# Second half of q copied by ScalarE alone, and one of two barriers at the program's end left out

## Chip, cores, metric

One core of one Trainium2 chip. The metric is the device time of one execution in microseconds, as the median of several runs; the profile's span runs from the first to the last instruction of the program and is some 1.8 us shorter.

## The reference

A decode step: one token for each of four sequences. Layer norm, then attention with 32 heads over the last 2048 rows of a cache, and a gated feed-forward block beside it. Cut to what matters:

```python
x = A_x                                   # (4, 1, 640)
xn = _layernorm(x, axis=-1)
# _A_ref: q = xn @ wq; W = 2048, Dh = 192, 32 heads
k = k_cache[:, :, Sk - W:, :]; v = v_cache[:, :, Sk - W:, :]
scores = jnp.einsum("bhqd,bhkd->bhqk", q, k) * (Dh ** -0.5)
o = jnp.einsum("bhqk,bhkd->bhqd", softmax(scores), v)
# ... o @ wo
# _B_ref: silu(xn @ w1) * (xn @ w3) @ w2
return x + _A_ref(xn, ...) + _B_ref(xn, ...)
```

K, V and the weights are 223 MB in bf16, each byte used once.

## The kernel before

All large loads go out from one sequencer (SP) in a fixed order. K has two buffers, so the load for head h+2 waits until VectorE has multiplied all of head h:

```python
def load_k(h):
    kt = kpool.tile([P, NJ, Dh], BF16, tag="kt")          # KBUFS = 2
    nc.sync.dma_start(out=..., in_=k_win[:, h]...)
```

q is projected in two halves of six 512-column blocks, in six PSUM banks; each half is copied to SBUF by ScalarE and VectorE in turn:

```python
for c0 in range(0, NQ, 6):                                # NQ = 12
    qps = [...six PSUM tiles...]
    ...                                                   # PE: 5 x 6 matmuls
    for i, qp in enumerate(qps):
        dst = qbc[:, (c0 + i) * QC:(c0 + i + 1) * QC]
        if i % 2:
            nc.vector.tensor_copy(out=dst, in_=qp[:])
        else:
            nc.scalar.copy(out=dst, in_=qp[:])
for i in range(2):                                        # banks of blocks 2 and 3
    o_ps = ps_o.tile([P, 2 * Dh], FP32, tag="o_ps", name="o_ps")
    nc.vector.memset(o_ps[:], 0.0)
...
def mult(u):                                              # VectorE, 128 times
    nc.vector.tensor_tensor(out=pr[:], in0=kts[h][:, ...], in1=qbc[:, h * Dh:(h + 1) * Dh]..., op=ALU.mult)
```

Behind the kernel's last instruction the framework puts an end block. From the program's listing, shortened (four engines signal POOL, which releases them; each barrier is eleven instructions):

```text
SP    drain, waits for all engines and all DMA queues
ACT/PE/DVE/SP  drain, gather+1 ; wait release      first barrier
POOL  drain ; wait gather>=4 ; release+4
POOL  drain ; EVENT_SEMAPHORE_RANGE_CLEAR
ACT/PE/DVE/SP  drain, gather+1 ; wait release      second barrier
POOL  drain ; wait gather>=4 ; release+4
```

Of the kernel before, what the change touches and what calls it, by code (L numbers as in the profile page):

```python
# [34 lines left out]
def first_load_first(nc):  # L35


    for f in nc.python_module().functions:
        head, body = f.blocks[0], f.blocks[1]
        sp = mybir.EngineType.SP  # L40
        i, ins = next((i, ins) for i, ins in enumerate(body.instructions)
                      if ins.engine == sp and not isinstance(ins, mybir.InstNoOp))
        assert isinstance(ins, mybir.InstDMACopy) and not ins.has_wait()
        j = next(j for j, other in enumerate(head.instructions)
                 if other.engine == sp and isinstance(other, mybir.InstDrain))
        del body.instructions[i]
        head.instructions.insert(j, ins)


@with_exitstack  # L50
def kernel(
# [19 lines left out]
    nc = tc.nc  # L71
# [26 lines left out]

    nc.at_finalize(keep_loaded_weights)
    nc.at_finalize(first_load_first)  # L100
    ctx.enter_context(tc.manual_schedule())
    head = ctx.enter_context(tc.tile_pool(name="head", bufs=1))
    fpool = ctx.enter_context(tc.tile_pool(name="ffn", bufs=1))
# [134 lines left out]
    for c0 in range(0, NQ, 6):  # L238
        qps = [pool.tile([P, QC], FP32, tag=tag, name="qps")
               for pool, tag in ((ps_add, "ps"), (ps_add, "ps"), (ps_o, "o_ps"), (ps_o, "o_ps"), (ps_m, "mt"), (ps_t, "t"))]  # L240
        for kc in range(KC):
            for i, qp in enumerate(qps):
                nc.tensor.matmul(qp[:], lhsT=xnT[:, kc].rearrange("p a b -> p (a b)"),  # L243
                                 rhs=wq_rows[kc][:, (c0 + i) * QC:(c0 + i + 1) * QC],
                                 start=(kc == 0), stop=(kc == KC - 1))
        for i, qp in enumerate(qps):
            dst = qbc[:, (c0 + i) * QC:(c0 + i + 1) * QC]
            if i % 2:
                nc.vector.tensor_copy(out=dst, in_=qp[:])  # L249
            else:  # L250
                nc.scalar.copy(out=dst, in_=qp[:])
# [322 lines left out]
```

## Time and profile before

| | before |
|---|---|
| time, median of 3 runs | 525.95 us (525.63 to 526.19) |
| span of the profiled run | 523.8 us |
| busy share PE / VectorE / ScalarE | 69% / 65% / 11% |
| DMA load queue busy | 99.2% |

The last pieces of the chain of waits (start, length, what):

```profile
489.68 30.66 DMA w<-in_B_w_dram
...
520.38 0.76 PE acc L264 x8
521.13 0.47 DVE res L542
```

The large last part of w2 (480 KB), issued at 489.68, lands at 520.34. Behind the loads come only the last sums, the result's copy, its store and the end block. The timeline's row of SP issuing the first K load that has to wait for a buffer:

```profile
41.62 0.54 SPq L125 DMA_DIRECT2D kt<-in_A_k_cache_dram  x1
```

### The profile page before, as it was taken

What the parts mean: (1) busy time and instruction counts of PE and PEld (TensorE: products, weight loads), DVE (VectorE), ACT (ScalarE), POOL (GpSimd) and SP (SyncE); (2) the same over time, 40 slices, a digit from 0 to 9 for tenths busy, and PEclk for the clock granted to TensorE, in tenths of its full rate; (3) what the DMA queues carried; (4) which work ended last, traced back from release to release, by engine and by line L of the source; (5) the groups of instructions that cost most, each with busy time, mean ns of one, the idle gap of its engine ahead of it and who ended that gap; (6) DMA issues with size and microseconds to landing.
All of it is one profiled execution on the core that took longest, in us unless ns stands there. A gap on an engine that the chain in (4) does not pass through costs nothing.

```text
span 523.8 us, 4820 instructions
## 1 busy us (share of the span) xinstructions
PE 361.8 (69%) x2336; PEld 75.9 (14%) x1643; DVE 340.9 (65%) x413; ACT 55.8 (11%) x176; POOL 5.6 (1%) x12
## 2 busy tenths in 40 slices
PE   0965866887668776667547768586686876675685
PEld 0100111121111111111111111111111111111122
DVE  3268853687656767577646877466667766667671
ACT  2111111111001110101100111001101110011111
POOL 4000000000000000000000000000000000000000
PEclk9979886898878998789997988889878898889988
DMA  9999999999999999999999999999999999999996
GB/s 389 422 443 425 433 431 432 428 433 432 430 435 428 437 418 446 424 437 426 434 434 429 432 434 429 435 427 435 425 437 434 427 437 431 430 434 425 441 418 275
DMA packets 11904, 223.26 MB, mean 426 GB/s; under 512 B 1332, under 2 KB 1608, under 8 KB 3052
## 3 DMA queue, kind: packets, MB, share of 16 engines
q1 hardware_dynamic: 11868, 222.96, 99.2%
q8 instruction: 15, 0.25, 0.2%
q14 instruction: 5, 0.04, 0.0%
q10 hardware_dynamic: 16, 0.01, 0.0%
HBM read 222.96 MB, written 0.01 MB: 426 GB/s over the span
## 4 chain that ended last, share of the span: by engine, by line
DMA 60%; PE 20%; DVE 15%; ACT 3%; issue 1%; SPq 1%
DMA kt<-in_A_k_cache_dram 44%; PE ps L288 11%; DMA w<-in_B_w_dram 11%; DVE pr L277 10%; DMA vt<-in_A_v_cache_dram 5%; PE po L361 4%; PE qps L243 3%; DVE sc L296 2%; ACT ex L324 1%; DVE z L332 1%; DMA x_sb<-in_A_x_dram 1%; PE mt L318 1%; ACT L324 0%; ACT negm L321 0%; PE mt L305 0%
## 5 line engine op out<-in xcount | busy, mean ns | idle before, releaser
L288 PE MATMUL ps<-pr,idb 128*128 128x512 bf16 x768 | 214.7, 422 | 137.6 <-DVE pr L277 137.5
L277 DVE TENSOR_TENSOR pr<-kt,qbc 128x3072 bf16<-128x3072 bf16 x128 | 223.5, 1746 | 104.0 <-DMA kt<-in_A_k_cache_dram 104.0
L296 DVE TENSOR_REDUCE sc<-ps 128x16 f32<-128x512 f32 x128 | 87.1, 681 | 2.7 <-PE ps L288 2.6
L340 PE MATMUL o_ps<-vt,z 128*8 128x384 bf16 x1024 | 60.5, 380 | 0.2 <-DVE z L332 0.2
L361 PE MATMUL po<-o_sb,sel_w 128*32 128x192 f32 x128 | 49.2, 518 | 0.6 <-ACT o_sb L343 0.6
L340 PEld LDWEIGHTS <-z 128*8 128x8 bf16 x1024 | 26.2, 95 | 98.8 <-issue 89.2
L332 DVE TENSOR_TENSOR z<-ex,mask_b 128x256 bf16<-128x256 bf16 x32 | 13.5, 423 | 38.6 <-ACT ex L324 38.6
L343 ACT COPY o_sb<-o_ps 128x384 f32<-128x384 f32 x32 | 15.3, 478 | 196.9 <-PE o_ps L340 196.9
L313 ACT ACTIVATE gneg<-gmax 1x128 f32<-1x128 f32 x32 | 9.8, 308 | 162.8 <-DVE gmax L310 162.8
L305 PEld LDWEIGHTS mt<-idf,lmax 128*1 128x1 f32 x32 | 3.2, 101 | 127.5 <-issue 125.5
L361 PEld LDWEIGHTS po<-o_sb,sel_w 128*32 128x32 f32 x128 | 13.8, 130 | 29.4 <-issue 27.9
L288 PEld LDWEIGHTS <-idb 128*128 128x128 bf16 x124 | 12.0, 97 | 39.3 <-issue 32.8
L318 PEld LDWEIGHTS mt<-ones_ff,gneg 1*128 1x128 f32 x64 | 9.6, 186 | 47.1 <-issue 43.7
L243 PE MATMUL qps<-wt,xnT 128*128 128x512 bf16 x59 | 14.9, 412 | 0.1
L318 PE MATMUL mt<-ones_ff,gneg 1*128 1x1 f32 x64 | 12.3, 259 | 0.7 <-ACT gneg L313 0.7
L321 ACT COPY negm<-mt 128x1 f32<-128x1 f32 x32 | 5.1, 159 | 70.4 <-PE mt L318 70.4
L310 DVE TENSOR_REDUCE gmax<-mt 1x4 f32<-1x128 f32 x32 | 8.8, 274 | 5.8 <-PE mt L305 5.8
L348 PEld LDWEIGHTS po<-rsum,tot_w 128*32 128x32 f32 x64 | 4.4, 108 | 51.5 <-ACT ex L324 35.4
L249 DVE CAST qbc<-qps 128x512 bf16<-128x512 f32 x6 | 3.8, 684 | 11.7 <-PE qps L243 11.7
L324 ACT ACTIVATE ex<-sc,negm 128x64 bf16<-128x64 f32 x32 | 11.1, 348 | 1.0
L305 PE MATMUL mt<-idf,lmax 128*1 128x128 f32 x32 | 10.9, 340 | 0.0
L199 PE MATMUL xnT_ps<-idb,xn 4*128 4x4 bf16 x5 | 0.4, 178 | 13.4 <-DVE xn L194 13.4
(74 smaller groups left out, 84.4 us busy)
## 6 DMA issues: line engine op xcount, KB each, us to landing
kt<-in_A_k_cache_dram SPq DMA_DIRECT2D x32, 3072.0 KB, 19.1
vt<-in_A_v_cache_dram SPq DMA_DIRECT2D x32, 3072.0 KB, 25.5
wo_t<-in_A_wo_dram SPq DMA_DIRECT2D x8, 960.0 KB, 20.7
wt<-in_A_wq_dram SPq DMA_DIRECT2D x2, 3072.0 KB
w<-in_B_w_dram SPq DMA_DIRECT2D x1, 1920.0 KB
wt<-in_A_wq_dram SPq DMA_DIRECT2D x1, 1536.0 KB, 19.5
w<-in_B_w_dram SPq DMA_DIRECT2D x1, 1536.0 KB
w<-in_B_w_dram SPq DMA_DIRECT2D x2, 640.0 KB
```

What stands on the lines that cost most here:

```text
L243: nc.tensor.matmul(qp[:], lhsT=xnT[:, kc].rearrange("p a b -> p (a b)"), rhs=wq_rows[kc][:, (c0 + i) * QC:(c0 + i + 1) * QC], start=(kc == ...
L277: nc.vector.tensor_tensor(out=pr[:], in0=kts[h][:, g * JQ:(g + 1) * JQ, :], in1=qbc[:, h * Dh:(h + 1) * Dh].unsqueeze(1).to_broadcast([P, ...
L288: nc.tensor.matmul(ps[:], lhsT=idb[:], rhs=pr[:, :, kk * DD:(kk + 1) * DD], start=(kk == 0), stop=(kk == NK - 1))
L296: nc.vector.tensor_reduce(out=scs[h][:, g * JQ:(g + 1) * JQ], in_=pss.pop(u)[:], axis=AX.X, op=ALU.add)
L305: nc.tensor.transpose(out=mt[0:1, 0:P], in_=chs[h][0][:], identity=idf[:])
L313: nc.scalar.activation(out=gneg[:], in_=gmax[:].unsqueeze(1).to_broadcast([1, PB, B]), func=ACTF.Copy, scale=-SCALE)
L318: nc.tensor.matmul(mt[:, P:P + 1], lhsT=gneg[:].rearrange("o p b -> o (p b)"), rhs=ones_ff[:], start=True, stop=True)
L324: nc.scalar.activation(out=ex[:], in_=scs.pop(h)[:], func=ACTF.Exp, bias=negm[:, 0:1], scale=SCALE, accum_out=rsum[:])
L332: nc.vector.tensor_tensor(out=z[:], in0=ex[:].unsqueeze(2).to_broadcast([P, NJ, B]), in1=mask_b[:].unsqueeze(1).to_broadcast([P, NJ, B]), ...
L340: nc.tensor.matmul(o_ps[c * CT:c * CT + 2 * B, :], lhsT=z[:, 2 * jj:2 * jj + 2, :], rhs=vt[:, 2 * jj:2 * jj + 2, :], start=(jj < 4), stop= ...
L343: nc.scalar.copy(out=o_sb[:], in_=o_ps[:])
L361: nc.tensor.matmul(po[sl, 0:Dh], lhsT=sel_w[:, par].rearrange("p a b -> p (a b)"), rhs=o_sb[:, par * Dh:(par + 1) * Dh].rearrange("p (r i) ...
```

## The change

Its intent: VectorE gets to its first multiply sooner, since ScalarE is idle there; and after the semaphores are cleared nobody has to meet again. The core of the diff:

```diff
+def one_end_barrier(nc):
+    for f in nc.python_module().functions:
+        end = f.blocks[2]
+        i = next(i for i, ins in enumerate(end.instructions) if isinstance(ins, mybir.InstISA))
+        keep = next(j for j in range(i + 1, len(end.instructions)) if end.instructions[j].engine == mybir.EngineType.Pool)
+        ...                                   # asserts
+        for j in range(len(end.instructions) - 1, i, -1):
+            if j != keep:
+                del end.instructions[j]
...
+    nc.at_finalize(one_end_barrier)
...
-            if i % 2:
+            if i % 2 and c0 == 0:
                 nc.vector.tensor_copy(out=dst, in_=qp[:])
             else:
                 nc.scalar.copy(out=dst, in_=qp[:])
```

More of the change, by code (lines that the diff above doesn't have):

```diff
@@ L47, in first_load_first @@
         head.instructions.insert(j, ins)
+def one_end_barrier(nc):
[3 more added lines that the diff above has]
+        keep = next(j for j in range(i + 1, len(end.instructions)) if end.instructions[j].engine == mybir.EngineType.Pool)
+        assert isinstance(end.instructions[keep], mybir.InstDrain)
+        for j in range(len(end.instructions) - 1, i, -1):
+            ins = end.instructions[j]
+            assert isinstance(ins, (mybir.InstDrain, mybir.InstEventSemaphore)), ins
+            if j != keep:
+                del end.instructions[j]
 @with_exitstack
```

## The prediction

> **What bounds the kernel now.** I read four views in this order: the page (bars and DMA queues), the stretches table, the DMA issues with the waits of the load-issuing sequencer, and last the instructions of the line that holds the program's end.
>
> First the bars and the queue, from the page:
>
> ```profile
> DMA  9999999999999999999999999999999999999996
> GB/s 389 422 443 425 433 431 432 428 433 432 430 435 428 437 418 446 424 437 426 434 434 429 432 434 429 435 427 435 425 437 434 427 437 431 430 434 425 441 418 275
> ...
> q1 hardware_dynamic: 11868, 222.96, 99.2%
> ```
>
> The reader should see that there is no slice, the ends apart, in which the 16 DMA engines rest. The load queue is busy 99.2% of the span, while the page gives PE 69%, DVE 65% and ACT 11%. Per stretch (columns: stretch, length, busy time and count of PE, PEld, DVE, ACT, POOL, then PE clock, DMA share, GB/s):
>
> ```profile
> 4.00:120.00 116.00, 81.37 (x493) 14.49 (x320) 72.27 (x94) 16.23 (x38) 4.23 (x3) 0.88 1.00 431
> 120.00:240.00 120.00, 83.06 (x506) 16.86 (x346) 81.69 (x94) 11.09 (x40) 0.00 (x0) 0.87 1.01 432
> ...
> 480.00:516.00 36.00, 25.02 (x195) 6.60 (x143) 21.67 (x27) 4.16 (x15) 0.00 (x0) 0.92 1.00 427
> 516.00:520.40 4.40, 3.16 (x48) 1.95 (x48) 0.80 (x2) 0.48 (x1) 0.00 (x0) 0.91 0.76 310
> 520.40:523.80 3.40, 0.69 (x8) 0.32 (x7) 0.48 (x1) 0.42 (x1) 0.00 (x0) 0.97 0.01 2
> ```
>
> From 4 to 516 us the share is 1.00 and the rate flat at 427 to 432 GB/s: 222.96 MB over 520.4 us is 428 GB/s. So the end of the loads is set by bytes over rate, and only 3.4 us of the span lie behind them. Is the queue ever about to run dry, so that an earlier issue would help? The issues (KB each, median us from issue to landing), then what the issuing sequencer waited for (total us, times, longest):
>
> ```profile
> kt<-in_A_k_cache_dram SPq DMA_DIRECT2D x32, 3072.0 KB, 19.1
> vt<-in_A_v_cache_dram SPq DMA_DIRECT2D x32, 3072.0 KB, 25.5
> ```
>
> ```profile
> SPq L125 <- DVE pr L277: 316.2, 30, 13.5
> SPq L125 <- DMA kt<-in_A_k_cache_dram: 73.4, 26, 5.7
> ```
>
> 3072 KB at 430 GB/s take 7.3 us, an estimate from the rate above. A K load lands 19.1 us after its issue, so typically 11.8 us of older loads are ahead of it. The sequencer waits 316 us for VectorE to free K buffers, which looks like a bound, but each time there is still work queued: this wait costs nothing unless it grows by about as much as that reserve.
>
> **What the skill says.** "DMA: Bandwidth & Descriptors", section "Where 436 GB/s comes from", puts the ceiling on the memory-side ports at 435 GB/s and says that about 358 binds for loads from HBM. The trace agrees with the first (431 to 432 sustained) and not with the second; the same page's "Measured" table has 425 for a single core. Either way no rate is left to gain. "Advanced Engine Details and Errata", section "The Read-Write Bubble", calls ScalarE closer to PSUM and VectorE closer to SBUF. The trace agrees in direction: for the same 128x512 copy out of PSUM, 592 ns on ACT against 681 ns on DVE. "Perfetto Trace Analysis", section "Sequencer-only Instruction (DRAIN, etc)", says that the profile shows only execution, not the semaphore wait or its propagation. So a barrier must be costed by start to start, not by summing its 7 to 51 ns rows. "Runtime: NRT & Kernel Launch", section "The ~15µs preamble/postamble breakdown", puts a synchronisation of all engines and a semaphore reset behind every kernel. The trace ends before these; the timed run beside the profile took 525.59 us for a span of 523.8, so 1.8 us lie outside it.
>
> **The change, part one: three copies from VectorE to ScalarE.** The instruction order shows the change is local: ACT has nine of these copies in place of six, DVE three in place of six, and nothing else moves in any engine's order. The second memset of the output banks now waits for ScalarE too, as does the first summing matmul. The place in the timeline (start, length, engine):
>
> ```profile
> 29.03 1.56 ACT L251 CAST qbc<-qps 128x512 bf16<-128x512 f32 x3 [5.11 <-PE qps L243]
> ```
>
> ```profile
> 29.25 1.89 DVE L249 CAST qbc<-qps 128x512 bf16<-128x512 f32 x3 [4.78 <-PE qps L243]
> 31.21 0.79 DVE L257 MEMSET o_ps<- 128x384 f32 x2
> 32.01 0.33 DVE L261 MEMSET acc<- 128x320 f32 x1
> 32.25 3.40 DVE L277 TENSOR_TENSOR pr<-kt,qbc 128x3072 bf16<-128x3072 bf16 x2
> ```
>
> Pace on ACT: (1.56 - 0.59) / 2 = 0.485 us from start to start; on DVE (1.89 - 0.68) / 2 = 0.605 us. PE delivers a finished column block every 0.22 us (the two engines' first copies start at 29.03 and 29.25), faster than either, so ACT alone sets the pace after the change. Its six copies start at 29.03 + 0.485 n: the fourth ends at 29.03 + 3 x 0.485 + 0.59 = 31.08 and the sixth at 32.05, where the six ended at 29.25 + 1.89 = 31.14 before. The set is thus finished 0.9 us later. But what VectorE needs is less: the two bank memsets need copies three and four only, and the first multiply reads the first head's 192 columns, copied in the first half. So the second memset starts near 31.14 in place of about 31.62 (31.21 plus one pace), and the first multiply near 31.77 in place of 32.25: VectorE gains about 0.48 us. It spends none of it: the first K reload is issued that much earlier into a queue that still holds old loads. DMA end: unchanged, 0.0 us.
>
> **Part two: the second barrier at the end.** It lies on the path, behind the output's landing. Rows of the program's last line from 523.3 us on, split at 523.6 us (durations min/median/max in ns, first and last start in us):
>
> ```profile
> L569 POOLq DRAIN  x2: 34/56/78, 523.3 to 523.5; - x2
> L569 PEldq EVENT_SEMAPHORE  x1: 51/51/51, 523.3 to 523.3; - x1
> ...
> L569 POOLq EVENT_SEMAPHORE_RANGE_CLEAR  x1: 96/96/96, 523.4 to 523.4; - x1
> ```
>
> ```profile
> L569 POOLq EVENT_SEMAPHORE  x2: 17/17/17, 523.6 to 523.7; - x2
> L569 SPq EVENT_SEMAPHORE  x1: 17/17/17, 523.7 to 523.7; - x1
> ...
> L569 PEldq EVENT_SEMAPHORE  x1: 51/51/51, 523.7 to 523.7; - x1
> ```
>
> The first release reaches all engines at 523.3; then POOL clears the semaphores at 523.41 to 523.51, drains at 523.54 to 523.57, and gathers and releases the second barrier, whose last row ends at 523.80 (hundredths from the trace's records). The change keeps the clear and POOL's drain behind it, and deletes the other engines' drains and all the semaphore rows behind. The span should therefore end at 523.57: a gain of 0.23 us. For the four other engines the end moves from about 523.75 to 523.33, 0.4 us, but POOL ends last. Sum of both parts: 525.95 - 0.0 - 0.23 = 525.72, so 525.7 us.
>
> **Rivals.** (a) The copies help more: a VectorE that starts 0.48 us earlier shifts the whole chain. For it: the chain of waits gives K loads 44% and multiplies 10%. Against: those K loads are waits for the saturated stream, and the end of the chain is a w2 load issued at 489.68 that lands at 520.34. Had this been right, the time would be 525.2. (b) The copies hurt: the last copies end 0.9 us later, and ScalarE next has work at 46.60 after 16.0 us of idleness, so nothing there can be pushed; only a delayed first summing matmul could bite, and it needs copies one and two, done at about 30.1, long before 34.04. If it did bite, 0.5 us of reserve out of some 11 would go; time 525.7 still. (c) The end work that the runtime adds waits on something else than the program's last engine: then the second barrier is hidden (525.95), or all 0.4 us that the other engines save are kept (525.5). (d) Another ordering of the DMA packets moves the rate by a tenth of a percent, which is 0.5 us either way and larger than the effect. The three runs of before spread over 0.56 us, so this is likely to hide the gain.
>
> **Range and chances.** 525.7 us as the centre; run scatter of about 0.3 on either side, and rivals (a) and (c) at 525.2 to 525.95, give 525.1 to 526.2. A change of over 2% would be 10.5 us, more than everything outside the stream (3.4 us behind the loads and 1.8 outside the span): chances 0.01 faster, 0.98 same, 0.01 slower.
>
> **What would show it.** Right: nine copies on ACT at a 0.485 us pace, the first multiply near 31.8 us, the last w2 load landing within 0.5 us of 520.3, DMA still 99% busy, and only one drain of POOL after the clear, 3.2 us behind that landing in place of 3.4. Wrong: the last landing moved by over 1 us, gaps in the DMA row between 30 and 60 us, or a difference in time of over 0.6 us between runs on one chip while the span changes by 0.23.

## The result, and the profile after

| | before | after |
|---|---|---|
| time, median of 6 runs each | 525.88 us (525.63 to 526.19) | 525.62 us (525.54 to 526.17) |
| span, profiled run | 523.8 us | 523.7 us |
| time outside the span, mean | 1.80 us (9 runs) | 1.91 us (6 runs) |

The ratio is the mean time of the changed kernel's fast runs over that of the other's of the same rounds, so not quite the ratio of the medians: 0.9997, interval 0.9984 to 1.001. No difference is resolved. Time outside the span is a run's time less its span; spans are given to 0.1 us, so one value is good to 0.05.

The page of after, bars and load queue:

```profile
DMA  9999999999999999999999999999999999999996
GB/s 391 420 443 421 435 431 428 437 427 429 431 435 428 433 424 445 422 434 432 434 432 433 428 435 434 430 429 432 431 435 432 429 435 430 433 432 429 435 422 276
...
q1 hardware_dynamic: 11868, 222.96, 99.3%
```

The same picture: nothing but the ends is unfilled. The end of the chain of waits:

```profile
489.85 30.65 DMA w<-in_B_w_dram
...
520.54 0.76 PE acc L279 x8
521.30 0.47 DVE res L557
```

The 480 KB load of w2 lands at 520.50 in place of 520.34: 0.16 us later, not sooner. The start, in the timeline (ScalarE, then VectorE, then SP):

```profile
30.41 3.03 ACT L266 CAST qbc<-qps 128x512 bf16<-128x512 f32 x6 [5.11 <-PE qps L258]
```

```profile
32.13 0.87 DVE L272 MEMSET o_ps<- 128x384 f32 x2 [6.28 <-ACT qbc L266]
33.01 0.33 DVE L276 MEMSET acc<- 128x320 f32 x1
33.24 3.40 DVE L292 TENSOR_TENSOR pr<-kt,qbc 128x3072 bf16<-128x3072 bf16 x2
```

```profile
42.47 0.54 SPq L140 DMA_DIRECT2D kt<-in_A_k_cache_dram  x1
```

Six copies stand on ScalarE, and VectorE, idle for 6.28 us, now waits for them. The first multiply comes at 33.24, a whole microsecond later than before. That isn't the change's doing: the projection itself ended later in this execution (first copy at 30.41 in place of 29.03). Counted from the first copy the multiply follows after 2.834 us in place of 3.216, so 0.38 us sooner. In all profiled runs but e8, which has copies of its own, this interval is 3.216 to 3.218 us with the old copies and 2.833 to 2.835 with the new, while the first copy starts anywhere from 28.85 to 30.83 us. Relative times are needed here; absolute ones mislead.

The end block of after from 523.6 us on:

```profile
L584 POOLq EVENT_SEMAPHORE_RANGE_CLEAR  x1: 96/96/96, 523.6 to 523.6; - x1
L584 POOLq DRAIN  x1: 34/34/34, 523.7 to 523.7; - x1
```

Only POOL is left, and its drain is the last row. From the sequencer's wake on the output's landing to the end of the span the records give 0.819 us before (522.981 to 523.800) and 0.597 after (523.147 to 523.744): 0.222 us saved in the span. But the time outside the span grew by 0.11, so about half of it is not in the time.

### The profile page after: what moved, and what is told of

Read it like the earlier page. It is cut to its first block, busy times and chain, and to the rows that moved or that the text cites. A ratio compares the mean times of both kernels' runs of the same rounds, so it can differ in the third digit from the quotient of the medians.

```text
span 523.7 us, 4813 instructions
## 1 busy us (share of the span) xinstructions
PE 358.9 (69%) x2337; PEld 74.5 (14%) x1643; DVE 339.2 (65%) x410; ACT 57.3 (11%) x179; POOL 5.6 (1%) x12
## 3 DMA queue, kind: packets, MB, share of 16 engines
q1 hardware_dynamic: 11868, 222.96, 99.3%
## 4 chain that ended last, share of the span: by engine, by line
DMA 60%; PE 19%; DVE 15%; ACT 3%; issue 2%; SPq 1%; DVEq 0%
DMA kt<-in_A_k_cache_dram 44%; PE ps L303 11%; DMA w<-in_B_w_dram 10%; DVE pr L292 10%; DMA vt<-in_A_v_cache_dram 5%; PE po L376 4%; DVE sc L311 2%; PE qps L258 2%; ACT ex L339 1%; DVE z L347 1%; DMA x_sb<-in_A_x_dram 1%; PE mt L333 1%; ACT L339 0%; ACT negm L336 0%; PE mt L320 0%
## 5 line engine op out<-in xcount | busy, mean ns | idle before, releaser
L303 PE MATMUL ps<-pr,idb 128*128 128x512 bf16 x768 | 217.3, 426 | 140.5 <-DVE pr L292 140.5
L355 PE MATMUL o_ps<-vt,z 128*8 128x384 bf16 x1024 | 53.4, 345 | 0.2 <-DVE z L347 0.2
L355 PEld LDWEIGHTS <-z 128*8 128x8 bf16 x1024 | 24.5, 89 | 95.2 <-issue 83.5
L258 PE MATMUL qps<-wt,xnT 128*128 128x512 bf16 x60 | 16.2, 438 | 0.0
L279 PE MATMUL acc<-wo_t,oT 128*4 128x320 bf16 x96 | 9.2, 298 | 1.3 <-DMA wo_t<-in_A_wo_dram 1.3
```

What stands on the lines that cost most here:

```text
L258: nc.tensor.matmul(qp[:], lhsT=xnT[:, kc].rearrange("p a b -> p (a b)"), rhs=wq_rows[kc][:, (c0 + i) * QC:(c0 + i + 1) * QC], start=(kc == ...
L303: nc.tensor.matmul(ps[:], lhsT=idb[:], rhs=pr[:, :, kk * DD:(kk + 1) * DD], start=(kk == 0), stop=(kk == NK - 1))
L355: nc.tensor.matmul(o_ps[c * CT:c * CT + 2 * B, :], lhsT=z[:, 2 * jj:2 * jj + 2, :], rhs=vt[:, 2 * jj:2 * jj + 2, :], start=(jj < 4), stop= ...
```

## The experiments

All kernels gave correct results. "Lost" is the loading time lost between 40 and 60 us: from the records of DMA packets, the sum over time of how far the packets in flight fall short of 16, over 16. "Outside" is the mean time outside the span; e12's holds one run of 2.45 among four of 1.88 to 1.94, e1's one of 2.02 among four of 1.79 to 1.89.

| run | time, us | before | ratio (95%) | outside, us | first K reload issued, us | lost, us |
|---|---|---|---|---|---|---|
| before (its trace) | | | | 1.80 | 41.62 | 0.07 |
| after | 525.62 | 525.88 | 0.9997 (0.9984 to 1.001) | 1.91 | 42.47 | 0.07 |
| e1 copies only | 525.79 | 525.86 | 0.9998 (0.9985 to 1.001) | 1.87 | 42.19 | 0.08 |
| e2 barrier only | 526.24 | 525.86 | 1.0007 (0.9995 to 1.002) | 2.19 | 40.67 | 0.06 |
| e3 ten more barriers | 530.39 | 525.86 | 1.0088 (1.0074 to 1.0101) | 2.32 | 43.14 | 0.34 |
| e4 POOL drains | 528.20 | 525.86 | 1.0044 (1.003 to 1.0057) | 2.10 | 42.56 | 0.11 |
| e5 one more multiply | 527.24 | 526.20 | 1.0015 (0.9997 to 1.0034) | 1.89 | 44.47 | 0.12 |
| e6 six more | 534.57 | 526.20 | 1.0162 (1.0143 to 1.0181) | 1.92 | 52.18 | 7.86 |
| e7 all copies ScalarE | 525.78 | 526.20 | 0.9995 (0.9974 to 1.0016) | 1.88 | 42.29 | 0.09 |
| e8 second half VectorE | 526.62 | 526.20 | 1.0004 (0.9986 to 1.0022) | 1.84 | 44.89 | 0.62 |
| e9 barrier only, ACT padded | 525.70 | 525.74 | 0.9994 (0.998 to 1.0008) | 1.92 | 40.87 | 0.07 |
| e10 changed, DVE padded | 525.58 | 525.74 | 0.9991 (0.9976 to 1.0007) | 1.88 | 42.00 | 0.07 |
| e11 barrier only again | 526.01 | 525.74 | 1.0006 (0.9991 to 1.0021) | 2.17 | 43.26 | 0.21 |
| e12 three more | 528.94 | 525.74 | 1.0052 (1.0037 to 1.0067) | 2.02 | 47.75 | 3.06 |

The theory to test: the loads saturate, VectorE's start lies within a reserve of queued loads, and the barrier is on the path. The rivals: VectorE's start sets the end; the end work is hidden behind what follows the program.

### e1: the copies alone

```diff
-    nc.at_finalize(one_end_barrier)
```

> Only the three copies moved; both end barriers kept. Theory (loads saturate, the copies lie off the path): 525.9 us, within 0.3 us of before; from the landing of the last w2 load to the end of the span 3.46 us as before; first copy of the second half to first multiply 2.8 to 2.9 us in place of 3.22. Rival (the earlier VectorE shifts the whole chain): 525.4 us.

The first multiply came 2.834 us after the first copy, as expected, and the time was 525.79 against 525.86. The runs can't exclude 0.4 us by themselves (interval to 0.9985). The profiled run's span was 0.5 us longer than before's, with its 480 KB load of w2 only 0.07 us later. From the landing of the output's store to the end it took 0.819 us, exactly before's. The expected 3.46 us from that w2 load to the end were missed (3.85), because here the loads weren't what ended last. Some pieces of the chain of waits, from the last K load on:

```profile
478.96 18.12 DMA kt<-in_A_k_cache_dram
...
514.36 2.62 PE o_ps L354 x32
...
520.03 1.57 PE acc L278 x20
```

The chain goes through the work of the last head, whose sums, and w2's behind them, occupy PE until 521.55 in place of before's 521.09. The store is issued 0.46 us later (522.14 against 521.69) and itself takes as long (1.305 us to the sequencer's wake, 1.295 before). The same holds in e7 and e11; in the other traces the chain ends with w2's load. So the loads and the last head's work end close together, and either can be last.

### e2: the barrier alone

```diff
-            if i % 2 and c0 == 0:
+            if i % 2:
```

> Only the second barrier left out; copies as before. Theory: from the last w2 landing to the end of the span 3.23 us in place of 3.46, time 525.65 us, i.e. 0.2 us less, hardly above the scatter of the runs. Rival (the work after the program hides it): span 0.23 us shorter but the time unchanged, so the part of the time outside the span grows from 1.8 to 2.0 us.

A surprise. The end block took 0.596 us in place of 0.819 (522.942 to 523.538), as expected, but the time came out at 526.24, and the part outside the span rose not to 2.0 but to 2.19 us in every one of five runs (2.14 to 2.23). By this the barrier left out alone costs about 0.39 - 0.22 = 0.17 us net, an estimate: the times by themselves (interval 0.9995 to 1.002) don't resolve it. Nothing in either theory says so; e9 to e11 take it up.

### e3: ten more barriers

```diff
+    for _ in range(10):
+        nc.all_engine_barrier()
```

> The kernel before with ten more barriers of the same kind behind the second, to lift the cost of one out of the scatter. Theory (the barrier is on the path, 0.33 us per repetition from the records: gather 523.14, release 523.22, wakes to 523.28, drains done 523.44): span and time both 3.3 us longer, 529.2 us. Rival (hidden behind the runtime's end work): span 3.3 us longer, time 0 to 1 us longer.

The added line's rows (count, durations min/median/max ns, first and last start):

```profile
L572 POOLq EVENT_SEMAPHORE  x20: 17/17/17, 525.2 to 528.8; - x20
...
L572 ACTq DRAIN  x10: 8/8/136, 525.1 to 528.6; - x10
...
L572 PEldq DRAIN  x10: 8/8/128, 525.2 to 528.7; - x10
```

Eight of the ten follow each other at 0.326 to 0.328 us from gather to gather; the rows themselves take 7 to 51 ns, the rest is waiting that no row shows. Two take 0.66 and 0.60 us, and the two outliers above, a drain of ACT with 136 ns and one of PE with 128, are the late arrivals. Sum: 3.88 us in the span. Another 0.5 us came outside it (2.32, from 1.84 to 2.55), together 4.4, and the time rose by 4.53. So a barrier is fully in the time: the rival (hidden, 0 to 1 us) is out. The 3.3 us were too low by the two late repetitions and by the 0.5 us outside the span. (The profiled run is longer by another 1.25 us, since its w2 load lands at 521.59; see under e5, e6, e12.)

### e4: POOL alone goes on

```diff
+    for _ in range(40):
+        nc.gpsimd.drain()
-            if j != keep:
+            if j != keep and not (ins.engine == mybir.EngineType.Pool and isinstance(ins, mybir.InstDrain)):
```

> The changed kernel with 40 more drains on POOL alone behind the semaphore clear, the other four engines being done. Theory (the program's end is its last engine): span longer by 40 times the pace of a POOL drain, 0.05 to 0.13 us each by the two drains seen, so by 2 to 5 us, and the time by as much within 0.3 us. Rival (the end is where the other engines are done): the span grows, the time stays at 525.6 us.

```profile
L587 POOLq DRAIN  x40: 34/34/34, 524.2 to 526.5; - x40
```

The drains follow at 0.061 us, 2.43 us in all, and the time is 528.20: 2.34 us above before, which has the second barrier, and 2.6 above the 525.6 expected of the changed kernel. The end of the program is its last engine, even where the other four have been done for over 2 us; the prediction's idea that the other engines' 0.4 us might count is out.

### e5, e6, e12: VectorE late on purpose

```diff
-        nc.vector.tensor_tensor(out=pr[:], ...)
+        for _ in range(N + 1 if u == 0 else 1):      # N = 1 (e5), 6 (e6), 3 (e12)
+            nc.vector.tensor_tensor(out=pr[:], ...)
```

> The changed kernel with the first multiply done twice into the same tile, so VectorE is 1.7 us late from 33 us on, over three times the 0.48 us that the moved copies should save. Theory (there is a reserve of queued loads: those issued before the first K reload have landed by 46.4 us, the reload is issued at 41.6 us in the trace of before and 42.5 in that of after, so 3.9 to 4.8 us, less about 2 us to start a load): time 525.6 us, unchanged. Rival (VectorE's start shifts the end): 527.3 us.

> The same with six more multiplies, 10 to 10.5 us late. Theory: the delay above the reserve of 2 to 4.8 us is lost for good, since the queue runs dry once near 47 us: 5.5 to 8.5 us longer, 531 to 534 us, with a hole in the DMA row near 47 to 55 us. Rival 1 (VectorE's start shifts the end): 536 us. Rival 2 (reserve of 11.8 us, as the prediction used it from the median time to landing): unchanged, 525.6 us.

> The changed kernel with the first multiply done four times, 5.1 us late. From the run with six more (first K reload issued at 52.2 us, 7.9 us of loading time lost between 40 and 60 us) the reserve ends where the reload is issued at 44.4 us. Theory (a dry queue costs what lies beyond): reload at 47.0 to 47.8, 2.6 to 3.4 us lost there, time 528.2 to 529.2 us on a chip where before takes 525.9. Rival (whole shift): 531 us; rival (reserve of 11.8 us): 525.6 us.

The stretches table around the hole, e6 first, then e12 (the last two columns are DMA share and GB/s):

```profile
44.00:48.00 4.00, 3.36 (x8) 0.10 (x1) 2.83 (x3) 0.00 (x0) 0.00 (x0) 0.50 0.49 203
48.00:52.00 4.00, 3.22 (x11) 0.00 (x0) 3.98 (x4) 0.00 (x0) 0.00 (x0) 0.82 0.00 0
52.00:56.00 4.00, 2.98 (x13) 0.18 (x2) 3.96 (x6) 0.00 (x0) 0.00 (x0) 1.00 0.57 205
```

```profile
44.00:48.00 4.00, 2.86 (x12) 0.00 (x0) 4.00 (x4) 0.00 (x0) 0.00 (x0) 0.93 0.49 200
48.00:52.00 4.00, 2.79 (x13) 0.18 (x2) 3.97 (x5) 0.00 (x0) 0.00 (x0) 1.00 0.88 297
```

In e6 the DMA row is empty from 48 to 52 us. The loads issued before the first K reload have all landed by 46.4 us (before's records). The reload's first packets start 1.38 us after its issue in e6 (at 53.56) and 1.35 in e12, where e5's expectation put about 2. With the engines' gradual stop and start the gap counts for more: by e6's loss 46.4 + 7.9 - 52.2 = 2.1 us. The same figure gives 47.75 + 2.1 - 46.4 = 3.4 us for e12 (3.06 lost), 0.6 for e8 (0.62), 0.2 for e5 (0.12), and nothing for before and after. So the queue runs dry where the reload is issued at about 44.3 us; beyond, a microsecond late is about a microsecond lost, and it isn't won back: e6 is 8.4 us longer, e12 3.2 us by the medians and 2.7 by the ratio. Both rivals fall: with the whole shift e6 would have been 536 us and e12 531, with a reserve of 11.8 us both 525.6.

e5's time alone settles nothing: 525.74 to 528.58, while before ranged from 525.50 to 528.12. Its trace has only 0.12 us lost at the place in question, yet its 480 KB load of w2 lands 1.37 us later than before's. About half of that lies at the very end, where the 16 engines ran out unevenly (1.7 us lost after 516 us, 1.05 in before's trace).

The other half arises earlier, and shows that the count of packets in flight misses something. By it e3 and e11, whose reloads went out at 43.14 and 43.26, should have lost nothing, and yet they lost 0.34 and 0.21 us. The stretch from 46 to 50 us, after's trace first, then e3's (last column GB/s):

```profile
46.00:50.00 4.00, 2.35 (x12) 0.49 (x4) 3.68 (x4) 1.21 (x3) 0.00 (x0) 1.00 1.08 458
```

```profile
46.00:50.00 4.00, 2.76 (x14) 0.57 (x5) 3.99 (x5) 0.54 (x3) 0.00 (x0) 1.00 1.00 389
```

The DMA engines count as busy in both, but e3's move less. By the DMA records all 14 traces have loaded 19.00 to 19.05 MB by 46 us. By 60 us the eight with the reload by 42.56 us have 24.93 to 25.04 MB, and the four with it at 43.14 to 44.89 (e3, e5, e8, e11) 24.66 to 24.79: some 0.5 to 0.9 us behind at 430 GB/s, an estimate. They end behind, too: the 480 KB load of w2 lands at 520.29 to 520.89 in the eight, at 521.42 to 521.81 in the four. Why a thin queue moves less at a full share is not shown.

So being sooner can be worth something where the projection ends late. e3 and e11 have the old copies and their first copy at 30.40 and 30.53; after and e4 have the new ones and start at 30.41 and 30.49. Their w2 loads land at 521.59 and 521.81 against 520.50 and 520.89. That fits with the runs' times: of the 37 of before 9 took over 526.5 us, of the 20 of after, e1, e7 and e10 one. This was read from the traces afterwards; no run tests it, and no mean of the new copies is clear of the noise.

### e7, e8: the copies elsewhere

```diff
-            if i % 2 and c0 == 0:
+            if False:                     # e7
+            if i % 2 or c0 > 0:           # e8
```

> All twelve q copies on ScalarE. In the first half PE waits for the copies of a set before it fills it again: the sixth copy ends 0.9 us later than with two engines. Theory: V's first load and the first multiply are up to 1 us later, within the reserve: 525.6 us, same. Rival (the placement of the copies sets the end): over 526.4 us.

> The mirror of the change: the six copies of the second half all on VectorE, second barrier left out. Theory: six copies at 0.605 us end 29.25 - 0.22 + 5 x 0.605 + 0.68 = 32.74 in the times of before, so the first multiply is 1.6 us later than before and about 2.1 us later than in the changed kernel; within the reserve, 525.6 us, same. Rival: 527 us or more.

e7 is as expected: 525.78, nothing lost. e8's first multiply follows the first copy after 4.793 us, 1.96 later than in the changed kernel, close to the 2.1 expected. But with its reload at 44.89 us, e8 stands just over the edge at which the queue runs dry:

```profile
44.00:48.00 4.00, 2.31 (x11) 0.00 (x0) 3.96 (x6) 0.00 (x0) 0.00 (x0) 1.00 0.90 349
```

The 0.62 us lost there are in the trace; the time (526.62 against 526.20, ratio 1.0004) neither shows nor excludes them. "Within the reserve" was wrong by that much.

### e9, e10, e11: what e2 lost outside the span

e2 and the changed kernel have the same end block; they differ in three copies, hence in how many instructions ScalarE and VectorE have run when the program ends.

```diff
+    pad = const.tile([1, 1], FP32, name="pad")
+    for _ in range(3):                                   # e9, on e2
+        nc.scalar.copy(out=pad[:], in_=ones_ff[:])
+    for _ in range(2):                                   # e10, on the changed kernel
+        nc.vector.memset(pad[:], 0.0)
```

> Barrier left out, copies as before, and three 1x1 copies more on ScalarE in its idle time before the q copies, so that its instruction count is that of the changed kernel. The part of the time outside the span was 1.80 us for before, 1.91 for the changed kernel, but 2.19 with the barrier alone left out. Theory A (where an engine's last instructions lie in its instruction stream decides how soon it gets to what follows the program; ScalarE's position is the one): 1.9 us outside the span, time 525.7 us. Theory B (its position on VectorE, or the copies themselves): 2.2 us outside.

> The changed kernel with two 1x1 memsets more on VectorE, so that its count of instructions is that of the kernel with the barrier alone left out. Theory A with VectorE's position: 2.2 us outside the span. With ScalarE's position: 1.9 us, as the changed kernel. The span as the changed kernel's, 523.7 us.

> The kernel with the barrier alone left out, once more, with the two padded ones on the same chip. If its 2.19 us outside the span belong to the program: 2.1 to 2.3 again. If they belonged to that chip or hour: 1.8 to 1.95.

e11 repeats e2: 2.17 us outside (2.12 to 2.20 in six runs), on the same chip and in the same rounds in which e9 has 1.92 (1.88 to 1.96) and e10 1.88 (1.85 to 1.92). The ranges don't touch. Three tiny copies on ScalarE, in time in which it is idle, take 0.25 us off the end; two more instructions on VectorE do nothing. So the number of instructions that ScalarE has run matters, as theory A said beforehand, and neither the chip nor where q is copied does. That it acts by the place of the program's end in ScalarE's instruction stream is the reading that fits. The Trainium skill, "Runtime: NRT & Kernel Launch", section "Instruction fetch mechanics", tells of instruction blocks of 256 whose crossing is "mostly hidden". The profile does record fetches, as DMA packets of the kind "instruction"; e3's page has one more on each queue than before's (15 and 5):

```profile
q8 instruction: 16, 0.26, 0.2%
q14 instruction: 6, 0.05, 0.0%
```

By the packet records, e3's late drain of ACT, which ends at 526.49, is followed by one of 8192 bytes on q14 at 527.00, and the late one of PE, which ends at 527.74, by one of 16384 bytes on q8 at 528.27. That fits a crossing at both. For e2 it doesn't help: the last recorded fetch of e2 and e11 starts at 509.54 and 511.56, while e1 and e7, with a time outside the span of 1.87 and 1.88, have one 1.75 and 1.06 us behind the span's end. So why ScalarE's count of e2 is dear (183 instructions in the trace) while those of e8 (180), before (185) and after (186) are not stays open.

## Why the prediction was right

The time, 525.62 us, lies 0.1 from the predicted 525.7. That is less than the scatter of the runs, and "no change" would have passed as well, so the nearness itself is luck. By its steps:

- **The loads set the end; moving copies gains 0.0 us.** Held for the two profiled runs and within the scatter of e1: 99.3% busy, w2's landing within 0.16 us. e6 and e12 show how VectorE's start can reach the loads. But with the reload at 43.1 us or later the loads do end later (e3, e5, e8, e11), so that where the projection ends late the copies may gain; that isn't tested. And the loads aren't always what ends last (e1, e7, e11).
- **Copies: pace 0.485 us on ScalarE, 0.48 us sooner to the multiply.** The pace was 0.479 (30.410, 30.893, 31.370 and so on in the records). The gain was 0.38: I let the second memset start 0.06 us after ScalarE's fourth copy, and it took 0.153 (32.464 to 32.617). The check "first multiply near 31.8 us" failed outright at 33.24, because I took before's absolute times for fixed.
- **The reserve of 11.8 us.** Wrong as a number for this place. It came from the median time from issue to landing over the whole run. At the first K reload, the first place where the change can reach the loads, the queue would have run dry 2.7 us later in before's trace (44.3 - 41.62) and 1.8 in after's, and the rate sinks sooner still, where the reload comes at 42.56 to 43.14: 0.9 to 1.5 us later than before's. The conclusion stood because 0.4 us sooner needs no reserve; a change that had made VectorE 1.5 us later would have been mispredicted.
- **Second barrier: 0.23 us in the span.** Held: 0.222. "3.2 us behind the last landing in place of 3.4" held too: 523.744 - 520.50 = 3.24 and 523.80 - 520.34 = 3.46.
- **The 0.23 us carry over to the time.** This is the step that failed in part. I held the time outside the span fixed at 1.8 us; it became 1.91, so some 0.11 us of gain remain, and it hangs by the copies: with the barrier alone left out it becomes 2.17 to 2.19 and the gain turns into a loss of about 0.15, by the same estimate. Rival (c) had the right place but named only "hidden" or "more"; that it could depend on the instruction count of an engine was not in it.
- **The scatter hides it.** Held: runs of one kernel differ by 0.6 us and more. In the traces it goes with the moment of the first K reload and with how evenly the 16 engines run out after 516 us.

Why 0.1 us more lies outside the span when POOL ends last is not settled; e4, with POOL last by far, has 2.10, but e8, with POOL last as well, 1.84, and e1, with both barriers, 1.87. No version tried beats the others by more than the scatter: e9 and e10 end up with the changed kernel.

## What to carry to other kernels

Where one resource is filled throughout, ask of a change upstream how far the queue is filled at the very place it touches, not on average: here 0.4 us sooner left the time as it was within the scatter, 1.5 us later already took some of the rate, and from 2.7 us on each microsecond cost about one. Take times from the event before, not from the start of the span, when comparing two executions. And a gain of tenths at the program's end needs a look at the time outside the span, which can give it back or more.

## What the Trainium skill lacked or had wrong

- "DMA: Bandwidth & Descriptors", section "Where 436 GB/s comes from": its sentence that about 358 GB/s binds for loads from HBM can mislead when read alone, as the prediction read it: with one core running, 427 to 432 GB/s held from 4 to 516 us. The note under the same page's "Measured" table does say that 358 is for both cores of a pair streaming. Its ceiling of 435 agrees.
- "Runtime: NRT & Kernel Launch", "Instruction fetch mechanics": "mostly hidden" doesn't say that the end of a program can pay for its place in an engine's stream; three 1x1 copies on ScalarE changed the time outside the span from 2.17 to 1.92 us. That a fetch is the cause is not shown; the traces of the dear runs record none near the end.
- No page has the price of a barrier of all five engines that a program issues itself (the runtime page prices only the runtime's own): 0.327 us each in a row; or the pace of POOL's drains in a row, 0.061 us.
